# Pooled attention and a rational mixture layer on one core: blocks 0 and 1 run over d_ff in two halves, block 1's attention is brought up behind block 0's, and Newton's second step is written to PSUM

## The chip, the cores and the metric

The kernel runs on 1 core of one Trainium2 chip. The metric is the device time of one execution in microseconds (us); the median of the runs shown stands for a kernel. The engines are named as in the profile: PE (TensorE matmul), PEld (its weight load), DVE (VectorE), ACT (ScalarE), POOL (GpSimd) and SP (SyncE, which issues most DMAs here).

## The reference

All inputs are float32, except that the two weight matrices arrive as float64 words and are decoded on the chip.

```
q, k, v: (8 batches, 8 heads, 576 positions, 64)
k_p, v_p = mean over groups of 8 positions            # 72 keys per head
attn = softmax(q @ k_p^T / 8);  x = attn @ v_p        # x: 4608 tokens x 512
h = x @ w_in                                          # w_in: 512 x 2048
P = a0 + a1 h + a2 h^2 + a3 h^3
Q = 1 + |b0| |h| + |b1| h^2
out = (P / (Q + 1e-6)) @ w_out                        # w_out: 2048 x 512
```

## The kernel before, in words

The 4608 tokens are cut into 18 blocks of 256, and d_ff into 8 slices of 256. A **unit** (i, u) is block i on slice u. `mm1` (L403) makes h for it in 24 matmuls of 256 columns into a PSUM tile ph (two buffers); `rational` (L414) turns h into g on ACT, DVE and POOL; `mm2` (L448) adds g times w_out into the block's two PSUM sums po in 12 matmuls of 512 columns. `mm2` runs three units behind `mm1` (LAG). Both products are split: x, g and the weights are kept as a rounded part and a rest (gh and gl for g), and three of the four partial products are added.

The weights: slice u of either matrix is fetched as 1 MB of float64 words (`fetch`, `fetch_out`), and `decode` (L160) makes of it a float32 tile m and its two parts: one ACT operation (L166), two on DVE (L168, L171), one on ACT (L176), one on POOL (L177). There are 16 such decodes. Before, they are written beside block 0's eight units, one win and one wout with each.

The attention of a block has two tiles of 128 tokens (`attention`, L316): q is transposed (pq, qT), multiplied with the pooled keys (ps), reduced and exponentiated (mx, e, sm), transposed again (er, pm, pr into the maps am and ar), and `values` (L379) multiplies the maps with the pooled values (pv) into x. The pooled keys and values of a batch are made by `prep_k` (reduce ks on DVE, L233) and `prep_v` (adds on POOL, products vm and vr on DVE). This work of the next block is spread as `background` steps over the units of the block before it.

The order of the work is a list of units. Before: blocks 0 and 1 alternate with block 1 two units late, then blocks 2 to 17 follow one by one. The list is emitted by the loop at the end, and below it a scheduler puts the instructions of each engine into one queue, in which they run in order; only the opening, up to block 0's x, is written with a manual order. PSUM has two banks for ph, two for the attention and for r of blocks 0 and 1 (`ps_a`), and four in `ps_o`: po of blocks 0 and 1 take two each, and from block 2 on po takes two and r the other two (`po10`, `po11`).

`rational` divides by Q with a logarithm, an exponential and one Newton step. Its last lines before are these; r is PSUM, w and t are SBUF:

```
434  nc.vector.scalar_tensor_tensor(out=w, in0=w, scalar=QC,   in1=r, op0=ALU.add, op1=ALU.mult)
436  nc.vector.scalar_tensor_tensor(out=t, in0=t, scalar=na0,  in1=r, op0=ALU.add, op1=ALU.mult)
438  nc.vector.scalar_tensor_tensor(out=t, in0=w, scalar=-2.0, in1=t, op0=ALU.add, op1=ALU.mult)
```

So L438 reads two SBUF tiles. Lines L421 to L423 (ACT), L424 (POOL), L425 and L426 (DVE), L432 and L433 (ACT) come before, L440 (ACT, gh) and L441 (POOL, gl) after.

## Time and profile before

| | us |
|---|---|
| median of 3 runs | 1034.73 (1034.52 to 1034.81) |
| the profiled execution | 1034.07 |
| its span, first to last instruction | 1032.1 |
| PE busy | 970.7 (94%) |
| DVE busy | 796.0 (77%) |
| ACT busy | 703.6 (68%) |
| POOL busy | 537.7 (52%) |

The engines' busy times are unions of their instructions. The second part of the page cuts the span into 40 equal slices of 25.8 us, and a digit is a slice's busy share in tenths. [...]

### The profile page before, as it was taken

What the parts mean: (1) busy time and instruction counts of PE and PEld (TensorE: products, weight loads), DVE (VectorE), ACT (ScalarE), POOL (GpSimd) and SP (SyncE); (2) the same over time, 40 slices, a digit from 0 to 9 for tenths busy, and PEclk for the clock granted to TensorE, in tenths of its full rate; (3) what the DMA queues carried; (4) which work ended last, traced back from release to release, by engine and by line L of the source; (5) the groups of instructions that cost most, each with busy time, mean ns of one, the idle gap of its engine ahead of it and who ended that gap; (6) DMA issues with size and microseconds to landing.
All of it is one profiled execution on the core that took longest, in us unless ns stands there. A gap on an engine that the chain in (4) does not pass through costs nothing.

```text
span 1032.1 us, 16779 instructions
## 1 busy us (share of the span) xinstructions
PE 970.7 (94%) x6324; PEld 880.5 (85%) x6324; DVE 796.0 (77%) x1232; ACT 703.6 (68%) x1218; POOL 537.7 (52%) x456
## 2 busy tenths in 40 slices
PE   5746599979999999999999999999999999999998
PEld 5635499969999999999999999999999989999997
DVE  6799966687779876878876978698869885867564
ACT  3664766657866876766776677677767776767664
POOL 5577945255535743535753465347534743444443
PEclk9677699989999999999999999999999999999999
DMA  8952100131002300002300230013002200000000
GB/s 237 414 192 64 44 21 2 42 105 44 22 21 68 82 21 22 22 21 65 85 21 22 64 85 22 21 65 85 21 22 64 63 21 21 22 1 21 1 22 21
DMA packets 61872, 58.75 MB, mean 57 GB/s; under 512 B 40288, under 2 KB 40288, under 8 KB 61792
## 3 DMA queue, kind: packets, MB, share of 16 engines
q1 hardware_dynamic: 61792, 57.69, 18.3%
q8 instruction: 50, 0.82, 0.3%
q14 instruction: 30, 0.25, 0.1%
...
## 4 chain that ended last, share of the span: by engine, by line
PE 87%; DVE 7%; DMA 2%; issue 2%; POOL 1%; ACT 1%; SPq 0%; POOLq 0%; ACTq 0%
PE po L457 38%; PE ph L409 38%; PE pv L394 4%; PE ps L338 4%; DVE ks L233 2%; PE pq L323 1%; DMA rwout<-in_moe_w_out_dram 1%; PE pm L366 1%; DVE m_wout L171 1%; DMA st_v<-in_v_dram 1%; DVE er L361 1%; DVE m_win L171 0%; POOL st_v L199 0%; DVE t L438 0%; DVE m_win L168 0%
## 5 line engine op out<-in xcount | busy, mean ns | idle before, releaser
L409 PE MATMUL ph<-x,win 128*128 128x256 f32 x3456 | 460.7, 287 | 9.3 <-POOL win L177 3.4
L409 PEld LDWEIGHTS ph<-x,win 128*128 128x128 f32 x3456 | 442.5, 191 | 23.4 <-issue 4.3
L457 PE MATMUL po<-wout,gh 128*128 128x512 f32 x1152 | 369.9, 404 | 20.0 <-ACT gh L440 20.0
L424 POOL TENSOR_TENSOR w<-w,r 128x512 f32<-128x512 f32 x144 | 194.3, 1349 | 329.9 <-ACT r L423 322.7
L457 PEld LDWEIGHTS po<-wout,gh 128*128 128x128 f32 x1152 | 210.3, 191 | 60.2 <-ACT gh L440 21.8
L441 POOL TENSOR_TENSOR gl<-t,gh 128x512 fp32r<-128x512 f32 x144 | 193.1, 1341 | 98.5 <-issue 59.0
L457 PE MATMUL po<-wout,gl 128*128 128x512 f32 x576 | 228.0, 401 | 3.7 <-POOL gl L441 3.6
L434 DVE SCALAR_TENSOR_TENSOR w<-w,rp 128x512 f32<-128x512 f32 x144 | 98.3, 682 | 117.2 <-ACT rp L433 115.7
L432 ACT ACTIVATE rp<-w,cbias 128x512 f32<-128x512 f32 x144 | 99.9, 694 | 87.7 <-POOL w L424 81.7
L421 ACT ACTIVATE w<-ph 128x512 f32<-128x512 f32 x144 | 86.3, 599 | 89.3 <-PE ph L409 88.3
L457 PEld LDWEIGHTS po<-wout,gl 128*128 128x128 f32 x576 | 109.6, 190 | 29.5 <-POOL gl L441 5.1
L425 DVE TENSOR_TENSOR t<-t,ph 128x512 f32<-128x512 f32 x144 | 98.0, 681 | 43.1 <-ACT t L422 41.6
L440 ACT CAST gh<-t 128x512 fp32r<-128x512 f32 x144 | 89.4, 621 | 53.9 <-DVE t L438 53.4
L423 ACT ACTIVATE r<-w,abn 128x512 f32<-128x512 f32 x144 | 118.6, 823 | 2.1 <-POOL gl L441 2.0
L422 ACT ACTIVATE t<-ph,abn 128x512 f32<-128x512 f32 x144 | 112.2, 779 | 1.6 <-POOL gl L441 1.6
L438 DVE SCALAR_TENSOR_TENSOR t<-w,t 128x512 f32<-128x512 f32 x144 | 110.5, 768 | 2.2
L426 DVE SCALAR_TENSOR_TENSOR t<-t,abn,ph 128x512 f32<-128x512 f32 x144 | 106.8, 742 | 2.3
L436 DVE SCALAR_TENSOR_TENSOR t<-t,abn,rp 128x512 f32<-128x512 f32 x144 | 106.5, 740 | 0.0
L433 ACT ACTIVATE rp<-rp 128x512 f32<-128x512 f32 x144 | 84.0, 584 | 3.2
L199 POOL TENSOR_TENSOR st_v<-st_v 128x512 f32<-128x512 f32 (+1 forms) x48 | 54.9, 1148 | 23.8 <-DMA st_v<-in_v_dram 22.9
L233 DVE TENSOR_REDUCE ks<-st_k 72x128 f32<-72x1024 f32 x32 | 62.4, 1974 | 1.6 <-DMA st_k<-in_k_dram 1.6
L338 PE MATMUL ps<-kpT,qT 128*128 128x144 f32 (+1 forms) x320 | 48.1, 294 | 4.6 <-DVE e L343 3.8
...
## 6 DMA issues: line engine op xcount, KB each, us to landing
...
```

The lines of the kernel that those rows point to most:

```text
L409: nc.tensor.matmul(ph[:, f, :], lhsT=win[u][:, wi, (2 * c + f) * P:(2 * c + f + 1) * P], rhs=xs[xi][:, c, :], start=s == 0, stop=s == len( ...
L422: nc.scalar.activation(t, h, AF.Identity, bias=na2, scale=na3)
L423: nc.scalar.activation(r, w, AF.Identity, bias=b0, scale=b1)
L424: nc.gpsimd.tensor_tensor(out=w, in0=w, in1=r, op=ALU.mult)
L425: nc.vector.tensor_tensor(out=t, in0=t, in1=h, op=ALU.mult)
L426: nc.vector.scalar_tensor_tensor(out=t, in0=t, scalar=na1, in1=h, op0=ALU.add, op1=ALU.mult)
L432: nc.scalar.activation(r, w, AF.Ln, bias=cbias)
L434: nc.vector.scalar_tensor_tensor(out=w, in0=w, scalar=QC, in1=r, op0=ALU.add, op1=ALU.mult)
L436: nc.vector.scalar_tensor_tensor(out=t, in0=t, scalar=na0, in1=r, op0=ALU.add, op1=ALU.mult)
L438: nc.vector.scalar_tensor_tensor(out=t, in0=w, scalar=-2.0, in1=t, op0=ALU.add, op1=ALU.mult)
L441: nc.gpsimd.tensor_tensor(out=glf, in0=t, in1=ghf.bitcast(F32), op=ALU.subtract)
L457: nc.tensor.matmul(po, lhsT=g[:, f, ms], rhs=wout[u][:, wi, f * DM:(f + 1) * DM], start=(u == 0 and f == 0 and s == 0), stop=(u == NU - 1 ...
```

## The change

Line numbers of the changed kernel are some 10 higher: L168 and L171 are there L169 and L172, L361 is L372, L369 is L380, L397 is L408, L438 is L449.

- The weights' halves: `NA = NU // 2`. Blocks 0 and 1 run over slices 0 to 3 first, alternating with block 1 one unit late. Then come blocks 2 and 3 over slices 0 to 3 and over slices 4 to 7, then blocks 0 and 1 over slices 4 to 7, then blocks 4 to 17 as before. x of blocks 0 and 1 (2 x 512 KB each) is written to HBM and read back (`spill`, `reload`), and so are their half sums (512 KB each), which the last step adds on DVE.
- The decodes of slices 4 to 7 are written beside units 8 to 15 of the list (`todo`), those of slices 0 to 3 beside units 0 to 5; five slices are fetched at the start instead of three.
- In the manual opening the queries, scores and softmax of block 1 follow those of block 0, and block 1's `values` follow before the loop.
- v's eight small loads of batch 0 go out on ACT's queue, masks are made later.
- r of blocks 2 and 3 lies in `ps_a`, as does that of the first half of blocks 0 and 1.
- Newton's second step writes r (PSUM) instead of w, and the last step reads r and t: one SBUF tile instead of two.

```diff
@@ prep_v
-                    nc.sync.dma_start(
+                    queue.dma_start(                      # nc.scalar for batch 0
@@ rational
-        if i >= 2:
-            r = ps_o.tile([P, W], F32, tag=f"po1{u % 2}", ...)
-        else:
-            r = ps_a.tile([P, W], F32, tag="pa", ...)
+        if paired(i, u):                                   # i in (2, 3) or (i < 2 and u < NA)
+            r = ps_a.tile([P, W], F32, tag="pa", ...)
+        else:
+            r = ps_o.tile([P, W], F32, tag=f"po1{u % 2}", ...)
...
-            out=w, in0=w, scalar=QC, in1=r, op0=ALU.add, op1=ALU.mult)
-        nc.vector.scalar_tensor_tensor(
             out=t, in0=t, scalar=na0, in1=r, op0=ALU.add, op1=ALU.mult)
         nc.vector.scalar_tensor_tensor(
-            out=t, in0=w, scalar=-2.0, in1=t, op0=ALU.add, op1=ALU.mult)
+            out=r, in0=w, scalar=QC, in1=r, op0=ALU.add, op1=ALU.mult)
+        nc.vector.scalar_tensor_tensor(
+            out=t, in0=r, scalar=-2.0, in1=t, op0=ALU.add, op1=ALU.mult)
@@ new helpers
+    def spill(i, xs):
+        for s, x in enumerate(xs):
+            d = hbm.tile([P, NJ, TOK], F32, ...); nc.sync.dma_start(d, x.bitcast(F32))
+    def reload(i, kept):
+        xs = [work2.tile([P, NJ, TOK], F32R, tag=f"x{s}", ...) for s in range(2)]
+        for x, d in zip(xs, kept):
+            nc.sync.dma_start(x.bitcast(F32), d)
@@ mm2, end of a half
+        if i < 2 and u0:
+            part = stage.tile([P, 2 * DM], F32, tag="st", ...)
+            nc.sync.dma_start(part, parts.pop(i))
...
+                nc.vector.scalar_tensor_tensor(out=ob, in0=po, scalar=1.0 / WS, in1=ob,
+                                               op0=ALU.mult, op1=ALU.add)
@@ opening
+        step(t2)
+        step(t2, 2)
+        xs[0, 0] = values(0)
+        kept[0] = spill(0, xs[0, 0])
+        step(t3)
+        step(t3, 2)
...
+    xs[1, 0] = values(1)
+    kept[1] = spill(1, xs[1, 0])
@@ the list
-    LEAD = 2
-    for s in range(NU + LEAD):
-        ...
-    order += [(i, u) for i in range(2, NBLK) for u in range(NU)]
+    LEAD = 1
+    for s in range(NA + LEAD):
+        order += [(i, s - LEAD * i) for i in range(2) if 0 <= s - LEAD * i < NA]
+    order += [(i, u) for u0 in (0, NA) for i in (2, 3) for u in range(u0, u0 + NA)]
+    order += [(i, u) for i in range(2) for u in range(NA, NU)]
+    order += [(i, u) for i in range(4, NBLK) for u in range(NU)]
+    todo = {0: [("win", 2)], 1: [("wout", 1)], 2: [("win", 3)], 3: [("wout", 2)], 5: [("wout", 3)]}
+    for u in range(NA, NU):
+        for n, kind in enumerate(("win", "wout")):
+            todo.setdefault(2 * NA + 2 * (u - NA) + n, []).append((kind, u))
```

What the scheduler makes of this is seen in the engines' queues. In the rows, m_win2 is the tile of the decode of w_in's slice 2, t0_0 the t of unit (0, 0), ph, po, gh and rp likewise, and the last number is a buffer's.

DVE before, from the decode of slice 1 to the end of unit (0, 0):

```order
L168 TENSOR_SCALAR m_win1_372<-m_win1_372 128x1024
L171 SCALAR_TENSOR_TENSOR m_win1_372<-rwin1_183,m_win1_372 128x1024
L168 TENSOR_SCALAR m_win2_475<-m_win2_475 128x1024
L171 SCALAR_TENSOR_TENSOR m_win2_475<-rwin2_187,m_win2_475 128x1024
L425 TENSOR_TENSOR t0_0_408<-t0_0_408,ph0_0_383 128x512
L426 SCALAR_TENSOR_TENSOR t0_0_408<-t0_0_408,abn_98,ph0_0_383 128x512
L168 TENSOR_SCALAR m_wout1_482<-m_wout1_482 128x1024
L171 SCALAR_TENSOR_TENSOR m_wout1_482<-rwout1_185,m_wout1_482 128x1024
L434 SCALAR_TENSOR_TENSOR w0_0_409<-w0_0_409,rp0_0_419 128x512
L436 SCALAR_TENSOR_TENSOR t0_0_408<-t0_0_408,abn_98,rp0_0_419 128x512
L438 SCALAR_TENSOR_TENSOR t0_0_408<-w0_0_409,t0_0_408 128x512
```

DVE of the changed kernel, from the decode of slice 2 to the first step of the same unit:

```order
L169 TENSOR_SCALAR m_win2_585<-m_win2_585 128x1024
L172 SCALAR_TENSOR_TENSOR m_win2_585<-rwin2_186,m_win2_585 128x1024
L169 TENSOR_SCALAR m_wout1_668<-m_wout1_668 128x1024
L372 TENSOR_TENSOR er3_434<-e3_400,er3_434 128x64 x2
L172 SCALAR_TENSOR_TENSOR m_wout1_668<-rwout1_184,m_wout1_668 128x1024
L380 TENSOR_TENSOR am1_1_440<-pm3_449,am0_1_439 128x4x128
L169 TENSOR_SCALAR m_win3_766<-m_win3_766 128x1024
L172 SCALAR_TENSOR_TENSOR m_win3_766<-rwin3_190,m_win3_766 128x1024
L169 TENSOR_SCALAR m_wout2_849<-m_wout2_849 128x1024
L172 SCALAR_TENSOR_TENSOR m_wout2_849<-rwout2_188,m_wout2_849 128x1024
L436 TENSOR_TENSOR t0_0_540<-t0_0_540,ph0_0_515 128x512
L437 SCALAR_TENSOR_TENSOR t0_0_540<-t0_0_540,abn_100,ph0_0_515 128x512
```

Block 1's attention and the decodes up to wout2 now stand ahead of the first unit's first DVE step. Further on, the sixteenth decode (m_wout7) stands behind the fifth unit's last step in either kernel. DVE of the changed kernel there:

```order
L449 SCALAR_TENSOR_TENSOR t0_2_798<-rp0_2_809,t0_2_798 128x512
L372 TENSOR_TENSOR er4_825<-e4_734,er4_825 128x64 x2
L361 TENSOR_SCALAR sm5_746<-sm5_746 128x8
L445 SCALAR_TENSOR_TENSOR t1_1_885<-t1_1_885,abn_100,rp1_1_896 128x512
L447 SCALAR_TENSOR_TENSOR rp1_1_896<-w1_1_886,rp1_1_896 128x512
L362 RECIPROCAL sm5_746<-sm5_746 128x8
L436 TENSOR_TENSOR t0_3_1057<-t0_3_1057,ph0_3_1032 128x512
L169 TENSOR_SCALAR m_wout7_1786<-m_wout7_1786 128x1024
L449 SCALAR_TENSOR_TENSOR t1_1_885<-rp1_1_896,t1_1_885 128x512
L286 SCALAR_TENSOR_TENSOR vr1_110<-vs1_579,masks_98,vr1_110 128x2x64
L437 SCALAR_TENSOR_TENSOR t0_3_1057<-t0_3_1057,abn_100,ph0_3_1032 128x512
L172 SCALAR_TENSOR_TENSOR m_wout7_1786<-rwout7_858,m_wout7_1786 128x1024
```

What moved is the attention: that of block 2 (er4, sm5) is now among these rows, and before only that of block 1 was.

PE of the changed kernel, where block 3 hands its PSUM banks to r of block 0's second half; po3 sits in the banks that rp0_4 and rp0_5 take:

```order
L493 MATMUL po3_0_1_1773<-wout7_1790,gh3_7_2223 128x512 x2
L493 MATMUL po3_0_1_1773<-wout7_1790,gl3_7_2224 128x512
L420 MATMUL ph0_7_2539<-xr0_0_2061,win7_1713 128x256 x8
L420 MATMUL ph0_7_2539<-xr1_0_2062,win7_1713 128x256 x4
L420 MATMUL ph0_7_2539<-xr0_0_2061,win7_1713 128x256 x2
L349 MATMUL ps9_1_2445<-kpT0_103,qT9_2362 128x144 x2
L420 MATMUL ph0_7_2539<-xr0_0_2061,win7_1713 128x256 x6
L420 MATMUL ph0_7_2539<-xr1_0_2062,win7_1713 128x256 x4
L493 MATMUL po0_4_0_2605<-wout4_1401,gh0_4_2279 128x512 x2
```

Before, the same handoff was from block 1 to block 2; now it stands between block 3 and block 0's second half.

## Rows read from the trace of the kernel before

**Rows 1.** The page: span, busy time of the engines, and two lines of the 40 slices.

```profile
span 1032.1 us, 16779 instructions
PE 970.7 (94%) x6324; PEld 880.5 (85%) x6324; DVE 796.0 (77%) x1232; ACT 703.6 (68%) x1218; POOL 537.7 (52%) x456
...
PE   5746599979999999999999999999999999999998
...
PEclk9677699989999999999999999999999999999999
```

**Rows 2.** Busy time of each engine in four stretches; then granted clock, DMA share and GB/s.

```profile
22.70:123.70 101.00, 58.00 (x280) 49.84 (x280) 90.69 (x97) 61.91 (x95) 73.44 (x42) 0.70 0.54 194
123.70:203.00 79.30, 78.71 (x523) 71.35 (x524) 54.02 (x92) 52.44 (x90) 35.47 (x26) 0.97 0.08 21
203.00:231.00 28.00, 21.78 (x124) 19.23 (x123) 23.37 (x33) 16.43 (x33) 16.58 (x14) 0.82 0.30 91
231.00:1028.00 797.00, 797.00 (x5320) 727.44 (x5319) 613.08 (x991) 565.89 (x993) 398.74 (x326) 1.00 0.13 37
```

**Rows 3.** The chain of waits near the end: start, length, what.

```profile
986.21 2.85 PE ph L409 x24
989.05 2.78 PE po L457 x12
...
1017.18 11.25 PE po L457 x48
```

**Rows 4.** DVE in order of time, the evictions of block 2's and of block 15's first sum (13 blocks apart).

```profile
267.64 0.67 DVE L465 TENSOR_SCALAR ob<-po 128x512 f32<-128x512 f32 x1
...
942.74 0.68 DVE L465 TENSOR_SCALAR ob<-po 128x512 f32<-128x512 f32 x1
```

**Rows 5.** PE's matmul groups from the start to 124.2 us: count, busy, mean, idle before them.

```profile
L409 PE MATMUL ph<-x,win 128*128 128x256 f32 x168 | 29.3, 346 | 9.3 <-POOL win L177 3.4 <-ACT win L176 3.0 <-DVE t L426 3.0
L457 PE MATMUL po<-wout,gh 128*128 128x512 f32 x28 | 11.1, 513 | 17.4 <-ACT gh L440 17.4
...
L457 PE MATMUL po<-wout,gl 128*128 128x512 f32 x12 | 5.8, 529 | 3.7 <-POOL gl L441 3.6
```

**Rows 6.** PE in order of time at the last long wait of the opening.

```profile
119.92 2.08 PE L457 MATMUL po<-wout,gh 128*128 128x512 f32 x4 [7.89 <-ACT gh L440]
124.29 2.07 PE L457 MATMUL po<-wout,gh 128*128 128x512 f32 x4 [2.30 <-ACT gh L440]
```

**Rows 7.** DVE's groups from 22.7 to 123.7 us, the costliest and those that the sum needs.

```profile
L171 DVE SCALAR_TENSOR_TENSOR m_wout<-rwout,m_wout 128x1024 int32<-128x1024 int32 x8 | 14.2, 1769 | 0.2
L168 DVE TENSOR_SCALAR m_wout<-m_wout 128x1024 int32<-128x1024 int32 x8 | 10.7, 1344 | 1.5 <-ACT m_wout L166 1.5
L171 DVE SCALAR_TENSOR_TENSOR m_win<-rwin,m_win 128x1024 int32<-128x1024 int32 x8 | 10.7, 1340 | 0.2
L438 DVE SCALAR_TENSOR_TENSOR t<-w,t 128x512 f32<-128x512 f32 x5 | 8.4, 1673 | 0.1
L233 DVE TENSOR_REDUCE ks<-st_k 72x128 f32<-72x1024 f32 x4 | 7.7, 1951 | 0.0
L168 DVE TENSOR_SCALAR m_win<-m_win 128x1024 int32<-128x1024 int32 x8 | 7.6, 947 | 3.4 <-ACT m_win L166 3.4
L361 DVE TENSOR_TENSOR er<-e,er 128x64 fp32r<-128x64 f32 x8 | 5.8, 759 | 0.1
...
L436 DVE SCALAR_TENSOR_TENSOR t<-t,abn,rp 128x512 f32<-128x512 f32 x5 | 3.7, 735 | 0.0
...
L350 DVE TENSOR_SCALAR sm<-sm 128x8 f32<-128x8 f32 x2 | 2.3, 1148 | 0.0
L342 DVE TENSOR_REDUCE mx<-ps 128x4 f32<-128x288 f32 x4 | 1.8, 450 | 0.1
L343 DVE TENSOR_TENSOR e<-ps,mx 128x288 f32<-128x288 f32 x4 | 1.8, 445 | 0.0
```

**Rows 8.** DVE in order of time: the first decode, with no POOL operation beside it.

```profile
27.47 0.69 DVE L168 TENSOR_SCALAR m_win<-m_win 128x1024 int32<-128x1024 int32 x1
28.19 1.23 DVE L171 SCALAR_TENSOR_TENSOR m_win<-rwin,m_win 128x1024 int32<-128x1024 int32 x1
```

**Rows 9.** DVE's groups from 123.7 to 215 us, after the last decode.

```profile
L438 DVE SCALAR_TENSOR_TENSOR t<-w,t 128x512 f32<-128x512 f32 x11 | 7.6, 691 | 0.2
...
L350 DVE TENSOR_SCALAR sm<-sm 128x8 f32<-128x8 f32 x4 | 1.6, 401 | 0.0
L397 DVE TENSOR_TENSOR x<-pv,x 128x512 fp32r<-128x512 f32 x2 | 1.4, 692 | 5.8 <-ACT x L396 5.8
...
L361 DVE TENSOR_TENSOR er<-e,er 128x64 fp32r<-128x64 f32 x6 | 1.0, 212 | 0.0
```

**Rows 10.** PE in order of time at the handoff from block 1 to block 2.

```profile
217.04 0.34 PE L374 MATMUL pr<-identr,er 128*128 128x128 f32 x1 [5.92 <-DVE er L361]
...
218.34 1.22 PE L457 MATMUL po<-wout,gh 128*128 128x512 f32 x2 [0.30 <-ACT gh L440]
```

**Rows 11.** The chain of waits: block 2's values on PE.

```profile
179.14 0.67 PE pv L394 x6
...
182.07 2.65 PE pv L394 x26
```

**Rows 12.** A stretch of the opening, columns as in rows 2: DMA share and GB/s stand last.

```profile
22.70:41.70 19.00, 11.57 (x48) 9.86 (x48) 14.41 (x20) 12.07 (x24) 8.11 (x10) 0.64 1.03 408
```

More of the change, by code (lines that the diff above doesn't have):

```diff
@@ L268, in prep_v @@
         for c in range(3):
[L269 removed]
+            dst, st = vs[:, 2 * c:2 * c + 2, :] if c < 2 else vrs, sts[(c + 1) % 3] if sts else load(c)
             pool_rows(dst, st)
@@ L314, in load_q, with maps_of, attention @@
         qtiles[t] = qt
-    def attention(t, am, ar, bank):
+    maps = {}
+    def maps_of(i):
+        if i not in maps:
+            am = [work1.tile([P, NJ, TOK], F32R, tag=f"am{s}", name=f"am{s}_{i}")
+                  for s in range(2)]
+            maps[i] = am, work1.tile([P, 2, TOK], F32R, tag="ar", name=f"ar{i}")
+        return maps[i]
+    def attention(t, bank):
         sg = segs(t * P, P)
@@ L482, in prep @@
             yield from prep_v(n)
-    maps = {}
     def tiles(i):
-        am = [work1.tile([P, NJ, TOK], F32R, tag=f"am{s}", name=f"am{s}_{i}")
-              for s in range(2)]
-        ar = work1.tile([P, 2, TOK], F32R, tag="ar", name=f"ar{i}")
-        maps[i] = (am, ar)
-        banks = [bank_a, bank_h if i == 0 else bank_a]
-        return [attention(2 * i + m, am, ar, banks[m]) for m in range(2)]
+        banks = [bank_a, bank_h if i < 2 else bank_a]
+        return [attention(2 * i + m, banks[m]) for m in range(2)]
     def attend(i):
@@ L530, in tile_pooled_attention_then_rational_moe @@
         fetch_out(0)
-        for u in range(1, 3):
+        fetch(1)
+        load_scalars()
+        fetch_out(1)
+        for u in range(2, FETCHED):
             fetch(u)
@@ new lines, in tile_pooled_attention_then_rational_moe, with run_of, background @@
+    order += [(i, u) for u0 in (0, NA) for i in (2, 3) for u in range(u0, u0 + NA)]
+    order += [(i, u) for i in range(2) for u in range(NA, NU)]
+    order += [(i, u) for i in range(4, NBLK) for u in range(NU)]
+    def run_of(i, u):
+        return (i, 1) if i < 2 and u >= NA else (i, 0)
+    first, runs = {}, []
+    for at, (i, u) in enumerate(order):
+        if run_of(i, u) not in first:
+            first[run_of(i, u)] = at
+            runs.append(run_of(i, u))
+    def background(run):
+        i, again = run
+        if again:
+            xs[run] = reload(i, kept.pop(i))
+            yield
@@ L578, in conv @@
             return
-        drain(load(u))
-    def background(i):
         yield from prep(i)
         yield from attend(i)
-        xs[i] = values(i, *maps.pop(i))
+        xs[run] = values(i)
         yield
-    EARLY = 3
-    conv(load_wout, 0)
-    for u in range(1, CA):
-        conv(load_win, u)
-    for u in range(1, CB):
-        conv(load_wout, u)
-    cur, gen, done = 1, background(1), 0
+    todo = {0: [("win", 2)], 1: [("wout", 1)], 2: [("win", 3)], 3: [("wout", 2)],
+            5: [("wout", 3)]}
@@ L594, in tile_pooled_attention_then_rational_moe @@
+    for u in range(NA, NU):
+        for n, kind in enumerate(("win", "wout")):
+            todo.setdefault(2 * NA + 2 * (u - NA) + n, []).append((kind, u))
+    fetches = {2 * n: u for n, u in enumerate(range(FETCHED, NU))}
+    EARLY = 3
+    drain(load_wout(0))
+    drain(load_win(1))
+    cur, done = 2, 0
+    gen = background(runs[cur])
     pend = []
     for at, (i, u) in enumerate(order):
-        while i not in xs:
+        while run_of(i, u) not in xs:
             next(gen)
             done += 1
-        if i == 0:
-            if WIN_AT + u < NU:
-                fetch(WIN_AT + u)
-                fetch_out(WIN_AT + u)
@@ L603, in tile_pooled_attention_then_rational_moe @@
-        ph = mm1(i, u, xs[i])
-        pend.append((i, u, *rational(i, u, ph)))
-        while cur < NBLK:
-            steps = 17 + (10 if prep_at.get(cur) else 0)
-            start = max(0, first[cur] - EARLY - NU)
-            stop = max(start + 1, first[cur] - (EARLY if cur > 1 else 0))
+        if at in fetches:
+            fetch(fetches[at])
+            fetch_out(fetches[at])
+        ph = mm1(i, u, xs[run_of(i, u)])
+        pend.append((i, u, *rational(i, u, ph)))
+        while cur < len(runs):
+            n, again = runs[cur]
+            steps = 1 if again else 17 + (10 if prep_at.get(n) else 0)
+            start = max(0, first[runs[cur]] - EARLY - (1 if again else NU))
+            stop = max(start + 1, first[runs[cur]] - (EARLY))
```

109 lines of the change are left out of this document (64 added, 45 removed).

## The prediction, made before the changed kernel ran

> **What bounds the kernel now.** I read the page's 40 slices first [rows 1]: PE is full from the eighth slice to the end and not before, and the granted clock sits at 0.6 to 0.7 in the first five slices. The stretches sharpen that [rows 2]: from 231 us on PE is busy 797.00 of 797, so the rest of the program is bound by PE alone, at full clock. A block's period there is (942.74 − 267.64) / 13 = 51.93 us [rows 4]; a unit is 2.85 + 2.78 = 5.63 us [rows 3], eight are 45.04, so a block's attention costs PE 6.89. Eighteen blocks are 934.7 us of PE. PE's last matmul ends at 1017.18 + 11.25 = 1028.43 [rows 3]. So PE loses 93.7 us in all, by waiting or by running at half clock, and nothing but those 93.7 can change, since PE's work is the same in both kernels.
>
> Where are they lost? By the last long wait, at 124.3 us [rows 6], PE has done 168 mm1 matmuls (7 units, 19.95 us at full clock), 40 of mm2 [rows 5] (3.33 units, 9.3) and two attentions (13.8): 43.0 us of work, 81.3 lost. Of the other 12.4, some 10 lie in the stretch from 203 to 231, where PE is busy 21.8 of 28 at a clock of 0.82 [rows 2]: block 1 hands its banks to block 2's r, and a transposition waits 5.92 us for er [rows 10]. The last 2 are the restart: four mm2 matmuls take 2.07 [rows 6] rather than 0.93.
>
> In the lossy stretch, 22.7 to 123.7, DVE is busy 90.69 of 101 us and POOL 73.44 [rows 2]. All 16 decodes and five units' Newton steps pass DVE there, and its operations are slow while POOL works: L438 takes 1.67 us against 0.69 later, er 0.76 against 0.21, L350 1.15 against 0.40 [rows 7, 9]. So **the opening is bound by DVE**, and it ends when the last decode and the Newton step behind it are through.
>
> **The change, part by part.** The landmark is the DVE end, D, from which PE has work without a gap. The halves promise decodes that are spread out, but the listing shows the scheduler pulling all 16 forward: the last (m_wout7) still stands behind the fifth unit's last step, as before. What moved ahead of it is attention, of blocks 1 and 2. Through the eighth unit's last step (t1_3), behind which the four units of the first half are through for both blocks and no decode is left, DVE has 59 instructions more than the 97 of the stretch before.
>
> - Attention, block 2's and the rest of block 1's: eight mx and eight e at 0.45 (7.2), six er at 0.76 (4.6), four L350 at 1.15 (4.6), three am at about 0.7 (2.1), ten smaller (5.2): 23.7 us [rows 7].
> - Newton: three units more and one unit's first two steps, 17 operations at about 0.71 (that of L436 is 0.735): 12.1.
> - One decode step, two vr, one eviction: 3.0.
> - L449 in place of L438: it reads PSUM and one SBUF tile, as L436 does, which took 0.735 in the same stretch [rows 7]; five times 1.673 − 0.735: −4.7.
>
> Sum 34.1. Durations there overlap a little (90.69 busy for 96.7 of summed groups, factor 0.94), so DVE's work is 90.7 + 32 = 122.7 at most. At the other end, a decode pair without POOL beside it takes 0.69 + 1.23 = 1.92 [rows 8] against 2.70 on average [rows 7], er 0.21, L350 0.40 [rows 9]: 0.94 x (130.8 − 16 x 0.78 − 14 x 0.55 − 6 x 0.75) = 100, where 130.8 is 96.7 + 34.1. POOL's work in the stretch grows less than DVE's, so it is beside DVE for some two thirds of the time rather than 73%, and a few er stand behind the last decode. I take 116, near the upper end, because the decodes themselves still run beside POOL.
>
> [...] L438, with two SBUF inputs, is the form that more than doubled [rows 7, 9], and L436 is the one that did not. [...]
>
> If L449 kept 1.67 all the same, eight would cost 7.5 us more and the time would be about 1036.
>
> [...] By the trace L438 took 0.69 uncontended and L436 0.735 [rows 7, 9], so 144 x 0.045 = 6.5 us of DVE time over the run. That lies beside PE, which waits for nothing after 231 us [rows 2].
>
> DVE's idle: 10.3 us before. Now er and values of two more tiles ask for maps behind ACT; block 2's x alone waited 5.8 [rows 9]. Between 10 and 16 I take 14. With a start near 22, **D = 22 + 116 + 14 = 152 us**, bounds 130 to 160.
>
> PE's work ahead of D: 11 mm1 (31.35), 7 mm2 (19.5) and four attentions less block 3's values (27.6 − 3.3 [rows 11]) are 75.1; ph2_2 cannot start before D, since ph2_0's buffer is read just before it: 72.3. Lost by D: 152 − 72.3 = 79.7, against 81.3. Behind D come the restart (2) and handoffs. From block 3 to block 0's second half, po3 must be evicted before rp0_4 is written, then gh0_4 follows; in the listing PE has ph0_7 and the scores of tile 9 to run meanwhile, so I take 3; the reductions of a later batch, about 2 us each on DVE [rows 7], ahead of ph4_3 another 3. Six together, bounds 2 (fully covered) and 14 (worse than the 10 before). Total lost 79.7 + 2 + 6 = 87.7, against 93.7: **6.0 us saved**. The profiled execution took 1034.07, so 1028.1; it stands 0.66 below the median of the runs, so the forecast is **1028.7**.
>
> Costed at nothing, with the cover:
> - HBM traffic: 1 MB of x, at the 408 GB/s of the opening [rows 12], is 2.5 us; four mm1 and over five mm2, 27 us of PE's work, lie between the last mm1 that reads the old buffer and the first that reads the new. If that cover is gone it costs 2.5 plus latency per reload. The half sums return under four units.
> - SP's queue: the reload of block 1 waits for the last reader of its buffer, and k's load of batch 2 is queued behind; its consumers ks stand some 20 us later, with a slack of some 7.
> - Four evictions more beside PE; the tail's 48 matmuls are unchanged [rows 3].
> - v's loads on ACT's queue: a few us of issue before ACT has anything to do.
> - Block 1's attention ahead of the first unit: DVE reaches the unit's first step some 18 us later (the first mm1 near 50 rather than 32), but it is work that is needed anyway.
>
> **Rivals.**
> *The opening shrinks more.* For it: attention fills DVE's idle time and POOL is beside DVE less. Then the work is about 108, idle 10, D = 140, handoffs 4: lost 140 − 72.3 + 2 + 4 = 73.7, 20 saved, about 1015. Against it: decodes are still in one bunch. Chance 0.20.
>
> *The deferral is not real and the trade cancels.* All decodes stay early, which the listing shows; then the change only swaps which work precedes them: D near 157 and handoffs 7 give 93.7 lost again, about 1034.7. Chance 0.12.
>
> *Slower, by the first unit behind block 1's softmax and four decodes.* PE gets its first matmul of h only after them, its early work is all attention, and Newton's chain through POOL, ACT and DVE (ACT gh had PE wait 17.4 us before [rows 5]) starts late and runs one after another with DVE idle in each. With 8 to 10 us more idle, D = 162, and a handoff as dear as the present one (10): lost 162 − 72.3 + 12 = 101.7, 8 more than 93.7, so about 1043. It decides from the point where D and handoffs together pass 164 (93.7 + 72.3 − 2). For it: three separate waits of 2 to 8 us for gh and er already stand in the rows [rows 6, 10]. Against: DVE is 90% busy, so there is other work to run. Chance 0.26.
>
> **How the numbers follow.** The forecast's own case, 1020 to 1032.5, has what is left, 0.42. Runs of this kernel tell about 0.2% apart, some 2 us. Faster is the forecast and the first rival, 0.62; same 0.12; slower 0.26. The range leaves out a tenth at either side: down to 1012 (D near 137) and up to 1041 (D near 161 with the handoff of before).
>
> **What would show it.** Right: t1_3's L449 ends at 145 to 158 us; L449 takes about 0.74 in the opening; all decodes are over before it; PE waits for gh, ph's reader and er until there and is gapless behind it but for a few us where block 3 hands over; no matmul waits for a reload. Wrong: PE clock below 1 for a whole slice after 231 us, a matmul waiting for xr or a DMA, or PE's loss after D above 14 us; or D below 135, which would mean that contention and not the amount of work set DVE's time.

## The result, and the profile after

The changed kernel takes 1044.79 us (median of 4 runs, 1044.60 to 1045.37) against 1034.77 before: a ratio of 1.0098, 95% interval 1.0080 to 1.0115, 10 us slower. The forecast was 1028.7, 6 us faster, with a range of 1012 to 1041.

The page of the changed kernel, with the lines that answer to [rows 1]:

```profile
span 1042.9 us, 16811 instructions
...
PE 972.1 (93%) x6324; PEld 879.6 (84%) x6324; DVE 797.3 (76%) x1236; ACT 702.8 (67%) x1218; POOL 524.9 (50%) x456
...
PE   5367579999898999999999999999999999999998
...
PEclk8687789999999999999999999999999999999999
```

PE is busy for 1.4 us more in a span that is 10.8 us longer; nearly all that was added is waiting. Its slices show two places: the first six, one more than before, and two dips at the eleventh and thirteenth. The stretches say it in numbers (columns as in [rows 2]):

```profile
22.00:165.10 143.10, 92.06 (x515) 79.85 (x513) 120.99 (x158) 85.76 (x138) 91.08 (x55) 0.77 0.45 157
133.00:152.40 19.40, 16.52 (x122) 14.95 (x121) 10.39 (x18) 8.25 (x15) 3.66 (x2) 0.99 0.12 28
160.00:231.00 71.00, 71.00 (x458) 64.27 (x457) 48.58 (x74) 51.74 (x87) 33.09 (x26) 1.00 0.08 30
258.00:281.00 23.00, 19.77 (x114) 16.63 (x113) 16.84 (x29) 14.83 (x28) 13.37 (x13) 0.93 0.42 124
318.00:340.00 22.00, 19.27 (x121) 16.66 (x120) 19.85 (x33) 12.30 (x22) 10.57 (x10) 1.00 0.31 104
340.00:1040.00 700.00, 698.74 (x4659) 637.17 (x4657) 530.41 (x863) 493.57 (x869) 339.80 (x285) 1.00 0.12 36
```

The first line ends where the eighth unit's last step (t1_3) ends, the prediction's landmark D: 165.1 us rather than 152. DVE is busy 120.99 us up to it and idle 143.1 − 121.0 = 22.1. The second line is the place of the largest part of that idleness, 9.0 us: for 19.4 us DVE, ACT and POOL are busy for 10.4, 8.3 and 3.7 us, while PE still works. From 160 to 231 PE loses nothing. The fourth and fifth lines are the two handoffs, and behind them PE is gapless.

What happens from 133 to 155, engine by engine. POOL, in order of time: it finishes w of the sixth and seventh units (the second of them at 138.6) and then stands for 14.9 us.

```profile
130.10 1.33 POOL L435 TENSOR_TENSOR w<-w,r 128x512 f32<-128x512 f32 x1
...
137.33 1.29 POOL L435 TENSOR_TENSOR w<-w,r 128x512 f32<-128x512 f32 x1
153.51 1.15 POOL L363 TENSOR_TENSOR e<-e,sm 128x576 f32<-128x576 f32 x1 [14.89 <-DVE sm L362]
```

ACT, in order of time: the first step of r for these two units (L443) comes at 151.1 and 153.1 only, behind block 2's x (L407), block 3's qT (L338) and its e (L358).

```profile
142.20 0.59 ACT L407 CAST x<-pv 128x512 fp32r<-128x512 f32 x1 [1.32 <-PE pv L405]
...
144.54 0.59 ACT L338 COPY qT<-pq 128x512 f32<-128x512 f32 x1
...
150.51 0.68 ACT L358 ACTIVATE e<-e 128x576 f32<-128x576 f32 x1 [3.77 <-DVE e L354]
151.10 0.67 ACT L443 ACTIVATE rp<-w,cbias 128x512 f32<-128x512 f32 x1
...
153.13 0.67 ACT L443 ACTIVATE rp<-w,cbias 128x512 f32<-128x512 f32 x1
```

DVE, in order of time: it waits in its own queue for the same chain.

```profile
142.82 0.69 DVE L408 TENSOR_TENSOR x<-pv,x 128x512 fp32r<-128x512 f32 x1 [4.12 <-ACT x L407]
...
152.49 0.74 DVE L445 SCALAR_TENSOR_TENSOR t<-t,abn,rp 128x512 f32<-128x512 f32 x1
...
164.42 0.69 DVE L449 SCALAR_TENSOR_TENSOR t<-rp,t 128x512 f32<-128x512 f32 x1
```

PE, in order of time: it lives on finished g meanwhile, and runs out. The first of its waits, 6.33 us up to 124.7, lies ahead of that place; the third ends it. The fourth line below is the handoff from block 3 to block 0's second half, the last two the one into block 4.

```profile
124.70 1.09 PE L378 MATMUL pm<-identr,e 128*128 128x128 f32 x4 [6.33 <-DVE t L449]
...
129.76 1.09 PE L378 MATMUL pm<-identr,e 128*128 128x128 f32 x4 [2.27 <-DVE t L449]
...
155.33 1.09 PE L378 MATMUL pm<-identr,e 128*128 128x128 f32 x4 [4.34 <-DVE t L449]
...
275.96 1.57 PE L493 MATMUL po<-wout,gh 128*128 128x512 f32 x4 [2.40 <-ACT gh L451]
...
329.07 3.09 PE L420 MATMUL ph<-x,win 128*128 128x256 f32 x24 [1.53 <-DVE t L437]
332.62 0.70 PE L493 MATMUL po<-wout,gh 128*128 128x512 f32 x2 [0.46 <-DVE part L509]
```

Behind the wait of 4.34 us that ends at 155.3, PE runs at a granted clock of 0.50, half of the full one, up to 160 us (columns as above):

```profile
155.00:160.00 5.00, 4.67 (x13) 3.89 (x14) 5.00 (x10) 2.80 (x8) 2.56 (x2) 0.50 0.00 0
```

So an attention in a lump (block 2's values, block 3's scores) stood in three engines' queues between one unit's Newton chain and the next.

### The profile page after: what moved, and what is told of

It is laid out like the page before. It is cut to its first block, busy times and chain, and to the rows that moved or that the text cites. A ratio compares the mean times of both kernels' runs of the same rounds, so it can differ in the third digit from the quotient of the medians.

```text
span 1042.9 us, 16811 instructions
## 1 busy us (share of the span) xinstructions
PE 972.1 (93%) x6324; PEld 879.6 (84%) x6324; DVE 797.3 (76%) x1236; ACT 702.8 (67%) x1218; POOL 524.9 (50%) x456
## 3 DMA queue, kind: packets, MB, share of 16 engines
q1 hardware_dynamic: 63424, 63.45, 19.4%
## 4 chain that ended last, share of the span: by engine, by line
PE 83%; DVE 6%; DMA 3%; POOL 3%; issue 3%; ACT 2%; SPq 0%; POOLq 0%; DVEq 0%; ACTq 0%
PE po L493 36%; PE ph L420 36%; PE pv L405 4%; PE ps L349 3%; DMA st_k<-in_k_dram 2%; PE pq L334 2%; PE pm L378 1%; DVE ks L234 1%; POOL st_v L200 1%; DMA qt<-in_q_dram 1%; DVE m_win L172 1%; POOL wout L178 1%; POOL win L178 0%; PE pr L385 0%; DVE m_wout L169 0%
## 5 line engine op out<-in xcount | busy, mean ns | idle before, releaser
L420 PE MATMUL ph<-x,win 128*128 128x256 f32 x3264 | 434.4, 286 | 5.6 <-DVE t L437 5.3
L420 PEld LDWEIGHTS ph<-x,win 128*128 128x128 f32 x3264 | 418.4, 191 | 19.6 <-ACT x L407 3.9
L435 POOL TENSOR_TENSOR w<-w,r 128x512 f32<-128x512 f32 x144 | 187.1, 1299 | 343.6 <-ACT r L434 333.5
L452 POOL TENSOR_TENSOR gl<-t,gh 128x512 fp32r<-128x512 f32 x144 | 188.6, 1310 | 81.5 <-ACT gh L451 42.8
L445 DVE SCALAR_TENSOR_TENSOR t<-t,abn,rp 128x512 f32<-128x512 f32 x144 | 106.6, 740 | 121.5 <-ACT rp L444 120.9
L443 ACT ACTIVATE rp<-w,cbias 128x512 f32<-128x512 f32 x144 | 99.5, 691 | 79.2 <-POOL w L435 76.8
L449 DVE SCALAR_TENSOR_TENSOR t<-rp,t 128x512 f32<-128x512 f32 x144 | 98.8, 686 | 2.1
L447 DVE SCALAR_TENSOR_TENSOR rp<-w,rp 128x512 f32<-128x512 f32 x144 | 99.2, 689 | 0.0
```

The source lines that it names most:

```text
L420: nc.tensor.matmul(ph[:, f, :], lhsT=win[u][:, wi, (2 * c + f) * P:(2 * c + f + 1) * P], rhs=xs[xi][:, c, :], start=s == 0, stop=s == len( ...
L435: nc.gpsimd.tensor_tensor(out=w, in0=w, in1=r, op=ALU.mult)
L443: nc.scalar.activation(r, w, AF.Ln, bias=cbias)
L445: nc.vector.scalar_tensor_tensor(out=t, in0=t, scalar=na0, in1=r, op0=ALU.add, op1=ALU.mult)
L447: nc.vector.scalar_tensor_tensor(out=r, in0=w, scalar=QC, in1=r, op0=ALU.add, op1=ALU.mult)
L449: nc.vector.scalar_tensor_tensor(out=t, in0=r, scalar=-2.0, in1=t, op0=ALU.add, op1=ALU.mult)
```

## The experiments

All times are medians beside runs of the kernel before on the same chip; the ratio is to those, with its 95% interval. To place a loss I use one measure throughout: **what PE has lost by a time t**, that is t less PE's finished matmuls at full clock: 2.85 / 24 us for one of mm1, 2.78 / 12 for one of mm2 [rows 3], and 0.113 for one of an attention's, which is the 6.89 us of a block's attention over its 61 matmuls. Since all matmuls of an attention count alike, it is rough, to some 2 us, between kernels that stand in different parts of one by then. The expectations were written with an attention counted some 1.8 us dearer: their 5.2, 3.3, 6.5 and 5.3 us are 5.8, 3.3, 7.8 and 5.5 by this measure.

```
lost by            100    130    160    200    230    280    340    400 us   time
before            67.1   85.1   84.7   84.4   94.1   94.3   93.9   93.5   1034.8
b_newton          66.7   83.2   82.8   83.8   92.1   92.3   92.2   91.5   1032.0
after             66.7   84.0   94.2   94.6   94.8  101.1  104.3  104.2   1044.8
a_oldnewton       65.5   85.0   96.5  106.0  106.1  106.7  115.6  119.6   1061.5
a_hand            67.4   84.0   94.4   95.1   95.1   98.4  104.8  105.6   1046.4
a_unpaired        67.7   84.0   88.7   95.4   95.6   95.7  100.4  100.1   1039.2
a_att3            66.7   84.0   88.0   97.7   97.8  102.9  107.7  108.4   1049.9
a_defer           68.9   73.3   85.4   96.4   96.6  102.0  107.0  107.2   1047.4
a_def_att3        69.4   73.4   80.5   97.7   97.6  103.2  110.2  110.2   1050.8
a_no3             67.0   84.0   88.4   88.5   88.5   94.4  101.9  101.5   1034.9
a_tmp2            64.2   82.6   93.6  100.5  100.4  102.5  110.0  111.7   1054.4
a_rsbuf           64.9   82.6   92.5   98.1   98.1  101.7  110.8  113.1   1051.7
a_whole           66.2   79.7   81.4   81.1   88.9   88.6   88.8   88.4   1028.7
a_whole_hand      66.0   79.5   81.2   81.0   86.6   86.6   86.3   86.1   1026.5
w_early           63.2   80.0   83.4   83.1   89.8   90.0   89.9   89.8   1030.2
w_bg1             73.6   86.7   87.7   88.4   96.3   96.4   96.1   95.6   1036.3
w_old             66.7   81.1   85.0   85.8   95.2   95.2   95.1   94.6   1035.3
```

The times are medians. The column at 400 repeats the differences of the profiled executions' times to 0.5 us, but for a_no3, which does one attention less.

### Taking the change apart

**b_newton**: before.py with the three changed Newton lines and nothing else.

> The kernel before with the changed Newton steps alone (second step to PSUM, last step reads PSUM and one SBUF tile). Theory A (the opening before is bound by DVE, and five last steps took 1.67 us there where 0.74 is to be had): 4 to 5 us less in the opening, so 1029 to 1031. Rival (DVE's time is not what ends the opening, the chain through POOL and ACT is): 1034.5 plus or minus 1, with the last step at 0.74 us all the same.

1032.0 us, ratio 0.9974 (0.9965 to 0.9984): 2.7 us gained, between the two. The last step took 0.69 us among the decodes, against 1.67 [rows 7] (DVE's group from 22.7 to 123.7 us):

```profile
L438 DVE SCALAR_TENSOR_TENSOR t<-rp,t 128x512 f32<-128x512 f32 x4 | 2.7, 685 | 0.1
```

Five times 0.98 are 4.9 us of DVE, of which 2.7 reached the end.

**a_oldnewton**: the changed kernel with the old lines.

```diff
+            out=w, in0=w, scalar=QC, in1=r, op0=ALU.add, op1=ALU.mult)
+        nc.vector.scalar_tensor_tensor(
             out=t, in0=t, scalar=na0, in1=r, op0=ALU.add, op1=ALU.mult)
         nc.vector.scalar_tensor_tensor(
-            out=r, in0=w, scalar=QC, in1=r, op0=ALU.add, op1=ALU.mult)
-        nc.vector.scalar_tensor_tensor(
-            out=t, in0=r, scalar=-2.0, in1=t, op0=ALU.add, op1=ALU.mult)
+            out=t, in0=w, scalar=-2.0, in1=t, op0=ALU.add, op1=ALU.mult)
```

> The changed kernel with the Newton steps of before. Theory A (DVE's work sets the opening): eight last steps at 1.4 to 1.7 us instead of 0.69, so 4 to 7 us more, 1048 to 1052. Rival (the changed kernel's DVE has 22 us idle in the opening, which takes the extra up): 1043.5 to 1046.

1061.5 us, 1.0259 (1.0244 to 1.0275): 16.7 us slower than the changed kernel, far beyond both theories. DVE's group from 22.7 to 172 us:

```profile
L449 DVE SCALAR_TENSOR_TENSOR t<-w,t 128x512 f32<-128x512 f32 x7 | 8.8, 1269 | 0.0
```

Seven steps, each 0.59 us longer than in the changed kernel, are 4 us. The order of the queues changed as well, and the loss comes in the lumps of the table (11 us by 200, 4 more by 400). Which of the moved rows costs what was not taken apart.

**a_whole**: no halves.

```diff
-    NA = NU // 2
+    NA = NU
...
-    order += [(i, u) for u0 in (0, NA) for i in (2, 3) for u in range(u0, u0 + NA)]
-    order += [(i, u) for i in range(2) for u in range(NA, NU)]
-    order += [(i, u) for i in range(4, NBLK) for u in range(NU)]
+    order += [(i, u) for i in range(2, NBLK) for u in range(NU)]
...
-        return i in (2, 3) or (i < 2 and u < NA)
+        return i < 2
```

and no spill or half sums, r of blocks 2 and 3 in the sums' other two banks as before, and the decodes written beside the first twelve units.

> The changed kernel without the halves: blocks 0 and 1 alternate over all eight slices with block 1 one unit late, nothing goes through HBM, blocks 2 and 3 follow one by one; block 1's attention in the manual opening, the Newton steps, the loads stay. Theory A (the loss is the halves': they bring the attentions of blocks 2 and 3 into the opening, where r waits behind them for the two attention banks, and they add two handoffs of 5.2 and 3.3 us in place of one): 1029 to 1034, and PE waits once, at the handoff from block 1 to 2. Rival (the loss is the early attention of block 1, which keeps the first unit back to 66 us): 1040 to 1046.

1028.7 us, 0.9944 (0.9929 to 0.9959). **The halves, with all that hangs on them, cost 16.1 us, and the rest of the change gains 6.** The same stretch from 133 to 152.4, and the one with the handoff from block 1 to block 2:

```profile
133.00:152.40 19.40, 19.23 (x128) 16.96 (x128) 11.57 (x21) 13.74 (x23) 10.12 (x8) 1.00 0.12 28
...
203.00:231.00 28.00, 22.90 (x141) 20.67 (x140) 23.02 (x31) 18.63 (x36) 15.83 (x16) 0.88 0.45 126
```

PE is busy here with mm1 and mm2, and ACT and POOL at 13.7 and 10.1 us keep the Newton chains going. By 160 us PE has lost 81.4, against 94.2 in the changed kernel: 12.8 of the 16.1. Of these 4.3 are lost by 130 us already, ahead of the lump; where they come from was not taken apart (w_early below, which has block 2's scores at that place, has not lost them). By the same measure the handoffs lose 5.8 (260 to 280 us) and 3.3 (320 to 340) there against 7.8 (200 to 230) here, and some 2 us are spread over the rest.

**w_bg1**: a_whole with block 1's attention in the background of the first units (in the opening `step(t2)`, `step(t3)` and their kin are gone, and the background begins with block 1).

> The version without halves, with block 1's attention in the background of the first units as in the kernel before, not in the manual opening. If bringing it up front is a gain: 1030 to 1034 (1032.0 is the kernel before with the changed Newton steps). Theory E taken literally (attention beside the first units costs, ahead of them it doesn't) says the same. Rival (the first unit at 66 us rather than 48 costs as much as it gives): 1027 to 1029.5.

1036.3 us, 1.0017 (1.0007 to 1.0026), slower than either expectation and 7.6 us slower than a_whole, so **bringing block 1's attention up is worth 7.6 us against this version**. It is not the placing of the kernel before: there block 1 came two units late and its attention had three units to stand beside, here it comes one unit late and has one. The second unit's last step starts at 97.8 us here and at 70.7 in b_newton, which has the old placing; against b_newton a_whole gains 3.3 us, with the new loads and the new list in it. What bringing it up is worth against the kernel before is therefore not shown by itself. Where the attention stays behind, PE has lost 73.6 rather than 66.2 by 100 us. Its long waits from 50 to 130 us (us in total, times, longest):

```profile
PE ps L349 <- ACT qT L338: 10.9, 1, 10.9
PE po L493 <- ACT gh L451: 8.7, 2, 5.7
PE pm L378 <- POOL e L363: 7.1, 2, 6.1
```

**w_old**: a_whole with the old Newton lines (diff as for a_oldnewton).

> The version without halves, with the Newton steps of before. If their worth is DVE time in the opening: 2 to 4 us, as in the kernel before (2.7), so 1031 to 1033. Rival (16.7 us as in the changed kernel, whatever the opening holds): 1042 or more.

1035.3 us, 1.0004 (0.9994 to 1.0013): worth 6.6 us here, neither 2.7 nor 16.7. The eight last steps (DVE's group from 22 to 150 us) took 0.69 us more each, 5.5 us of DVE:

```profile
L449 DVE SCALAR_TENSOR_TENSOR t<-w,t 128x512 f32<-128x512 f32 x8 | 11.0, 1372 | 0.1
```

### Where the halves lose

**a_unpaired**: blocks 2 and 3 one after the other, blocks 0 and 1 still in halves.

```diff
-        return i in (2, 3) or (i < 2 and u < NA)
+        return i < 2 and u < NA
...
-    order += [(i, u) for u0 in (0, NA) for i in (2, 3) for u in range(u0, u0 + NA)]
+    order += [(i, u) for i in (2, 3) for u in range(NU)]
```

> The changed kernel with blocks 2 and 3 one after the other over all slices (r in the sums' other two banks from block 2 on), blocks 0 and 1 still in halves. Block 3's attention moves out of the opening, block 2's stays in it, and one handoff (block 1 to block 2, right behind the opening) stands in place of two. Theory A (attention in the opening, where r shares its two banks, and the two later handoffs are the loss of 16 us against the version without halves at 1028.7): 1033 to 1038, about half of it back. Rival (block 2's attention alone does it, or the first half's short run of eight units): 1041 or more.

1039.2 us, 1.0046 (1.0031 to 1.0061): 5.6 us back, a little less than expected. By 160 us 88.7 are lost, about halfway between the two. By 200 us the handoff from block 1 to block 2, which follows here at once, has taken that back (95.4 against 94.6); the kernel ends lower because it loses nothing more up to 280 us.

**a_no3**: block 3's attention left out (its x is block 2's).

> The changed kernel with block 3's attention left out (block 3 takes block 2's x). PE's work falls by one attention, 6.9 us. If that attention costs nothing but its work: 1037 to 1039. Theory C or D (its place in the opening costs another 5.3 us, the difference of what PE has lost by 160 us in the changed kernel and in the version with blocks 2 and 3 one after the other): 1031 to 1034.

1034.9 us, 0.9999 (0.9990 to 1.0009), between the two: 9.9 us less, 6.9 for the work and 3.0 for the place. By 160 more than 5 us are there (88.4 against 94.2); behind the later handoffs less is left of them (101.5 against 104.2 at 400).

**w_early**: a_whole with block 2's scores, softmax and maps where the changed kernel has them.

```diff
+        while i == 2 and here[0] < 12:
+            yield
         xs[run] = values(i)
...
+            if n == 2:
+                start, stop = 0, 5
```

> The version without halves, with block 2's scores, softmax and maps placed where the changed kernel has them (ahead of the decode of slice 6, beside the third to fifth unit); its values and all else stay. Theory E (attention placed among the decodes and the first units' Newton steps costs PE some 5.5 us a block): 1032.5 to 1035.5. Rival (the place is free, the halves cost by their handoffs, HBM traffic and the short runs of units): 1028 to 1030.

1030.2 us, 0.9954 (0.9939 to 0.9968): 1.5 us slower than a_whole. **Theory E falls**: the place of one attention's scores costs 2.0 us by 160, not 5.5. In its stretch from 133 to 152.4 DVE is busy 15.8 us and POOL 10.2:

```profile
133.00:152.40 19.40, 18.43 (x119) 16.52 (x120) 15.77 (x23) 14.70 (x27) 10.22 (x8) 1.00 0.00 1
```

What the changed kernel has beyond it by 160 us are block 2's values (a_unpaired and a_no3: 88.7 and 88.4, 5 us more) and block 3's scores right behind them (94.2, 5.5 more). That is the lump from 133 to 152. These are steps between kernels that differ in more than one thing, so the sizes are rough and not shares of one cause.

**a_att3**: block 3's queries wait for the seventh unit's product.

```diff
+        if at == 7:
+            load_q(6, pend[-2][2])      # writes one element of gh into the tile first
+            load_q(7, pend[-2][2])
...
+            if n == 3:
+                start, stop = 7, 10
```

> The changed kernel with block 3's queries fetched only after the seventh unit's product, so that its attention stands behind the eighth unit's Newton steps on DVE rather than before the sixth's. Theory A (DVE's 13 us of waiting from 137 to 151 us comes from that attention in front of r): the opening 5 to 7 us shorter, 1037 to 1040. Rival (the attention meets r in the same two banks a few units later, and costs the same there): 1043 to 1047.

1049.9 us, 1.0143 (1.0117 to 1.0169). That is 5.1 us slower than the changed kernel, more than the rival said. The opening did get shorter (88.0 lost by 160), and the loss came back between 160 and 200 (97.7), with the same lump in front of later units. The first line is ACT's: r's first step (L448) starts when DVE's e (L359) has read the scores, and the two share nothing but the attention banks. The second is the wait on PE:

```profile
168.29 0.69 ACT L448 ACTIVATE rp<-w,cbias 128x512 f32<-128x512 f32 x1 [1.60 <-DVE e L359]
...
173.66 2.08 PE L498 MATMUL po<-wout,gh 128*128 128x512 f32 x4 [5.11 <-ACT gh L456]
```

**a_defer**: fetches of slices 4 to 7 wait for the products of later units, in the same manner, so that eight decodes leave the opening.

> The changed kernel with the fetches of slices 4 to 7 made to wait for a product of the units 4, 6, 8 and 10, so that eight of the 16 decodes really stand behind the sixth unit on DVE. Theory B (the volume of DVE's work in the opening sets its end, 121 us of it to 165 us): eight decodes, 23 us, leave it, and what PE loses falls by 10 to 20 us, 1026 to 1035. Theory A (the end is set by r waiting behind attention in two banks, and by chains): little, 1040 to 1045, the decodes then fall into units that have DVE time to spare.

1047.4 us, 1.0123 (1.0108 to 1.0138). By 130 us PE has lost 73.3, 11 us less than the changed kernel, and by 200 us all of it is lost again (96.4). The eight decodes stand from 122 to 195 us now, where DVE is busy 55.9 of the 70 us from 130 to 200. PE's waits on the way:

```profile
72.47 1.11 PE L385 MATMUL pm<-identr,e 128*128 128x128 f32 x4 [21.41 <-POOL e L370]
...
146.90 1.09 PE L385 MATMUL pm<-identr,e 128*128 128x128 f32 x4 [7.16 <-DVE t L456]
...
182.85 2.08 PE L500 MATMUL po<-wout,gh 128*128 128x512 f32 x4 [2.76 <-ACT gh L458]
```

So theory B's gain doesn't come: taking decodes out of the opening moves its loss behind it. Whether that is because the attentions of blocks 2 and 3 are still due by units 8 and 12, or because the decodes now stand beside them, this run doesn't separate.

**a_def_att3**: both at once.

> Both of the last two together: eight decodes and block 3's attention behind the opening. Theory A and B both expect less than either alone; if each acts by itself 1022 to 1033. Rival (what leaves the opening stalls units 8 to 15 instead): 1036 to 1045.

1050.8 us, 1.0152 (1.0137 to 1.0167): as the rival said, what leaves the opening stalls units 8 to 15, and by more than it said. The loss is 80.5 by 160 and 97.7 by 200.

**a_tmp2 and a_rsbuf**: a_rsbuf has r of nineteen units in SBUF, with buffers changed to make room; a_tmp2 is the control, with the buffers alone.

```diff
-    NRT = 5
+    NRT = 6
...
-    tmp = ctx.enter_context(tc.tile_pool(name="tmp", bufs=6 - 3))
+    tmp = ctx.enter_context(tc.tile_pool(name="tmp", bufs=2))
...
+    INSB = [(0, 3), (1, 2), (1, 3)] + [(i, u) for i in (2, 3) for u in range(NU)]      # a_rsbuf alone
+        if (i, u) in INSB:
+            pass
-        if paired(i, u):
+        elif paired(i, u):
```

(As built, INSB holds all eight slices of blocks 2 and 3, so 19 units; the expectation's "eleven" miscounts them.)

> Control for the next: the changed kernel with six buffers for t, w and r in place of five, and two in place of three for small temporaries; nothing else differs. Every theory: near the changed kernel's 1044.8, within 3 us.

> The control with r of eleven units ((0,3), (1,2), (1,3) and the first four slices and last four of blocks 2 and 3, so of the units 6 to 8 and of all of blocks 2 and 3) kept in SBUF rather than in the two attention banks; the three Newton steps of these units then read two SBUF tiles. Theory C (the attentions of blocks 2 and 3 and r of the units beside them wait for each other in the two banks, and that is what PE loses between 118 and 160 us): 4 to 9 us below the control. Rival D (attention at two blocks in eight units is too much for the chain through DVE, ACT and POOL whatever the banks): within 2 us of the control, or slower by the contention of the Newton steps.

The control took 1054.4 us, 1.0187 (1.0168 to 1.0205), 9.6 us slower than the changed kernel: a miss. qT shares the temporaries with evictions and now holds PE up (9.5 us before 123), but by 130 us the control has lost no more than the changed kernel. It loses 5 us between 160 and 165 us, behind a lump like the one above: POOL's w of the sixth and seventh units is ready at 134.5 and 140.4, and r's first step comes only behind block 3's e. ACT, in order of time, then PE:

```profile
157.53 0.67 ACT L443 ACTIVATE rp<-w,cbias 128x512 f32<-128x512 f32 x1
...
158.72 0.67 ACT L443 ACTIVATE rp<-w,cbias 128x512 f32<-128x512 f32 x1
...
164.88 1.09 PE L378 MATMUL pm<-identr,e 128*128 128x128 f32 x4 [8.31 <-DVE t L449]
```

a_rsbuf took 1051.7, 1.0163 (1.0148 to 1.0178), 2.7 below its control and between the two expectations. In the opening it does what theory C said. r's first step for the sixth to eighth units (L445, ACT) comes right behind POOL's w, and ahead of block 2's x; the stretch from 133 to 152.4 follows it:

```profile
136.11 0.72 ACT L445 ACTIVATE r<-w,cbias 128x512 f32<-128x512 f32 x1
...
143.01 0.72 ACT L445 ACTIVATE r<-w,cbias 128x512 f32<-128x512 f32 x1 [0.92 <-POOL w L435]
...
148.72 0.72 ACT L445 ACTIVATE r<-w,cbias 128x512 f32<-128x512 f32 x1 [1.53 <-POOL w L435]
...
133.00:152.40 19.40, 15.63 (x75) 12.09 (x76) 16.17 (x26) 13.84 (x27) 11.90 (x9) 0.84 0.00 1
```

DVE, ACT and POOL are busy for 16.2, 13.8 and 11.9 us where the changed kernel has 10.4, 8.3 and 3.7, the wait of 8.31 us is gone, and by 165 us PE has lost 92.7 rather than the control's 98.7. **So r of these units waits because it shares two banks with the attention.** The gain is lost again from 165 to 200 us (5.4, in the control 1.8) and from 280 to 300 us (9.4, in the control 6.9). DVE's groups from 130 to 260 us, with r in SBUF and, below, in a bank:

```profile
L447 DVE SCALAR_TENSOR_TENSOR t<-t,abn,r 128x512 f32<-128x512 f32 x19 | 16.8, 885 | 9.7 <-ACT r L446 9.7
L449 DVE SCALAR_TENSOR_TENSOR r<-w,r 128x512 f32<-128x512 f32 x18 | 16.4, 911 | 0.9
L451 DVE SCALAR_TENSOR_TENSOR t<-r,t 128x512 f32<-128x512 f32 x18 | 15.8, 878 | 0.3
...
L451 DVE SCALAR_TENSOR_TENSOR t<-rp,t 128x512 f32<-128x512 f32 x2 | 1.4, 676 | 0.0
```

Three steps with two SBUF inputs cost 0.55 us a unit more than with r in a bank (0.885 + 0.911 + 0.878 = 2.67 us, against 0.744 + 0.688 + 0.688 = 2.12 in the changed kernel from 130 to 260 us), 10.5 us of DVE over nineteen units. That they are what eats the gain is likely but **not shown**: no run frees the banks without them.

### The handoffs

**a_hand**: r of block 0's slices 4 and 5 in the attention banks.

```diff
-        if paired(i, u):
+        if paired(i, u) or (i == 0 and u in (NA, NA + 1)):
             r = ps_a.tile([P, W], F32, tag="pa", name=f"rp{i}_{u}")
```

> The changed kernel with r of block 0's units on slices 4 and 5 in the attention banks, so that they need not wait for block 3's sums to be evicted. Theory A (r of the unit waits 8.6 us for that eviction, and PE loses 5.2 us by it): 1039 to 1041.5. Rival (r then waits in the attention banks behind block 4's scores, and PE's restart at half clock stays): 1044 to 1046.

1046.4 us, 1.0113 (1.0098 to 1.0128): the rival, 0.4 us above its upper end. The loss at this handoff (260 to 300 us) falls from 5.7 to 4.5 us, and the next one rises from 3.3 to 5.4; PE's wait there (in the changed kernel 1.53):

```profile
328.84 4.59 PE L420 MATMUL ph<-x,win 128*128 128x256 f32 x24 [2.93 <-DVE t L437]
```

**a_whole_hand**: the same for block 2's first two units in a_whole (`or (i == 2 and u < 2)`).

> The version without halves (1028.7) with r of block 2's first two units in the attention banks, so that they need not wait for block 1's sums to be evicted; PE loses 6.5 us at that handoff. If the eviction is what costs: 1024 to 1027. Rival, as for block 0's second half in the changed kernel, where r met the next block's attention in those banks and 1.6 us were lost: 1028 to 1031.

1026.5 us, 0.9918 (0.9902 to 0.9935), the fastest of all: 2.2 us below a_whole and 8.4 below before. Its stretch of the handoff, against 22.90 busy at a clock of 0.88 in a_whole:

```profile
203.00:231.00 28.00, 24.34 (x154) 20.75 (x154) 24.33 (x37) 19.50 (x36) 16.66 (x16) 1.00 0.36 105
```

## Why the prediction was wrong

- **What bounds the kernel: right.** PE is gapless behind the opening and the handoffs, its work is unchanged, and the difference is waiting and the half clock behind a wait (0.50 from 155 to 160 us). One reading was off: PE's slices are full from the tenth on and not from the eighth, and the first slice has a clock of 0.9 [rows 1]; the sum doesn't use it.
- **The decodes stay bunched: right.** The sixteenth is through at 133.8 us, and the halves give none of the promised spread. Making the spread real (a_defer) doesn't help either.
- **The failing step is D = 22 + 116 + 14 = 152.** It was 165.1. DVE's work was 121.0 us, close to the 122.7 that the opening's own durations gave and not the 116 that I took. The idle time was 22.1 and not 14, and it is the worse error: I let the idle grow by less than 4 us, with one priced wait, that of block 2's x (5.8 before, 5.1 here), and overlooked that block 2's values, block 3's queries, scores and softmax stand behind each other in the queues of PE, ACT and DVE, all ahead of r of the sixth unit, which shares the attention's two banks (a_rsbuf, a_att3). I counted those rows' durations and not the waits between them; 9.0 us of DVE's idle time lie in that one stretch.
- **PE's work ahead of D**: 72.3 was forecast. At 165.1 us PE has done 10 mm1 (28.5), 76 matmuls of mm2 (17.6) and four attentions less some 3.8: 69.9. So 95.2 are lost where the forecast had 79.7 + 2.
- **Handoffs**: 5.8 and 3.3 against 3 and 3. The first is the wait that the prediction named: r of (0, 4) stands behind po3's eviction. POOL has its w at 261.9, and ACT's r begins 8.7 us later, released by the eviction (ACT, in order of time). The cover that I named, ph0_7 and scores, was too short:

```profile
270.56 0.69 ACT L443 ACTIVATE rp<-w,cbias 128x512 f32<-128x512 f32 x1 [1.38 <-DVE ob L514]
```
- The sum: 13.5 us in the opening and 3.1 in the handoffs, 16.6 together; 1044.8 − 1028.7 = 16.1. That a_whole took the 1028.7 of the forecast is chance: it is another kernel.
- **L449: right.** 0.684 us in the opening for a forecast of 0.735 (group of DVE from 22.7 to 172 us, the changed kernel):

```profile
L449 DVE SCALAR_TENSOR_TENSOR t<-rp,t 128x512 f32<-128x512 f32 x9 | 6.2, 684 | 0.1
```

Of the five old last steps in the opening of the kernel before, four took 1.47 to 2.82 us, each with POOL at work beside it (the longest at 50.16 us, over POOL's L177 from 50.03 to 52.43); the fifth, at 71.81 us with POOL idle, took 0.68. It was not so beside every POOL instruction: at 146.28 us, beside L424, the step took 0.68. L449 took 0.68 at 76.77 in the changed kernel although POOL's L178 ran all the while (76.15 to 79.07), and nowhere in the run more than 0.698; with the old lines a_oldnewton has 1.269 in its opening. The 0.045 us a step, 6.5 us over the run, that the prediction allowed for the step that reads PSUM doesn't show: L449 takes 0.686 over the whole run, and L438 with two SBUF inputs took 0.691 after the last decode [rows 9].
- **Costed at nothing, and rightly**: HBM traffic. PE waits for no reload; its only wait for a DMA is one of 2.6 us for q before 12 us. v's eight loads held ACT's queue for 9.67 us and not for a few, and ACT's first copy came at 10.58 us where it had come at 8.49; by 100 us PE has lost no more than before (66.7 against 67.1).
- **The slower rival** had the outcome (about 1043, from D and handoffs beyond 164; they are 165.1 + 9.1 = 174.2) and the kind of loss, DVE idle for 8 us more than forecast in a chain through the engines. It had the wrong place: it blamed block 1's attention ahead of the first unit, and a_whole, which keeps that, is 6 us faster than the kernel before. The lump was one block later.

What stays open: of the 16.1 us, 12.8 are lost by 160 us. Four kernels tie 8.5 of them to the values of block 2 and the attention of block 3, and a_rsbuf to the banks that r shares with them, but no run takes the banks alone out at no other cost; the 4.3 before 130 us have no cause yet. And why the Newton steps are worth 2.7, 6.6 and 16.7 us in three surroundings is only told in part, by the time that the old last steps took beyond 0.69 us in the opening (4.9, 5.5 and 4 us).
